# An S5 scan beside a gated MLP on one core: x tiles loaded first, transfers re-queued, and the first gate steps reordered

## The chip, the cores and the metric

The kernel runs on one core of one Trainium2 chip. The metric is the device time of one execution in microseconds; below, "us" always means that. Before the change the median of three runs is 185.41 us (185.02 to 185.9).

## The reference, cut to what matters

The input x has 2048 tokens of 448 features (bfloat16). Every token is layer-normalised to `xn`. Two branches start from `xn` and are multiplied at the end:

```
xn = layernorm(x)
h  = Lam_bar * h + xn @ B_bar.T            # complex state of 448, over the 2048 tokens
s  = 2*real(h @ C.T) + xn * Dskip
g  = silu( (sigmoid(xn @ w_gate) * (xn @ w_up)) @ w_down )      # 448 -> 1792 -> 448
out = x + s * g
```

## The kernel before, in words

**Tiles and stages.** Tokens are cut into 16 tiles of 128, and into 4 chunks of 512 (four tiles each). TensorE wants features on the partitions, so each normalised tile is transposed: in chunk 0 by TensorE itself (L495 `pe_transpose`: eight small matmuls into an accumulator `acc`, then one copy to `xnT`, by ScalarE for tile 0 and by VectorE for tiles 1 to 3), in the later chunks by DMA transposes that SyncE issues (L512). A chunk then runs through

- seven *gate steps* g0 to g6 and seven *up steps* u0 to u6 (L699 `gu_mm`): each has 7 pairs of matmuls, two halves of 64 rows side by side, into one of three double banks `gu0` to `gu2` of PSUM, taken in turn. ScalarE empties a gate step (Tanh, L721), VectorE an up step (L724). In chunk 0 all gate steps come before the up steps;
- the input side of the scan (L750 `b_phase`): it takes the next three `gu` banks and both `acc` banks. L764 and L761 are its first matmuls (part 3 into `acc`, then parts 0 and 1 into two `gu` banks), then L778 and L775; ScalarE copies the results to `bus` (L789, L795);
- the scan itself on VectorE (L826 `ssm_pair`, L862 `ssm_stack`), and the two output products `down` (L896) and `yout` (L914). Of chunk 1 on, `down` of the chunk before runs inside `b_phase`, in banks that `b_phase` has just emptied.

**Parameters.** `columns` (L535) turns three parameter rows, loaded by GpSimd, into columns with five tiny matmuls; VectorE copies them to `pv` (L546), and GpSimd and ScalarE make the scan's sine tables from it (`tables`, L570: ScalarE L575, VectorE L577 and L579, ScalarE L582 to L600). `c_scale` (L665) scales the C matrices: ScalarE L673 reads the transposed C and writes `ctmp`, VectorE L676 finishes. `skip_row` (L480) makes `xd = xn * dbc`, where `dbc` is Dskip broadcast to all partitions by a DMA.

**Loads, and names for them.** The gate weights come in three blocks for each half of the features: steps 0 and 1, steps 2 and 3, steps 4 to 6. I call them G0a, G0b, G0c for half 0 and G1a, G1b, G1c for half 1 (224, 224 and 336 KB). The up weights come in two blocks, steps 0 to 2 and 3 to 6: U0a, U0b, U1a, U1b (336 and 448 KB). A tile of x is 112 KB; "x4-7" is one DMA of four tiles. SyncE (SP) and ScalarE (ACT) issue them; every DMA of these two engines signals one of eight completion semaphores in turn, so the issue of a DMA waits for the landing of the one eight places before it. After its loads SP issues `dbc`, then the DMA transposes of B, of chunk 1's `xn`, the loads of w_down, the DMA transposes of C, and x of chunks 2 and 3.

**What sets the order.** The kernel is written down as a list of operations with costs, engines, reads and writes (L85 `add`). A planner (L138 `solve`) walks backward from TensorE's order for due times and then forward: each engine takes, of the operations that it thinks ready, the one due first. A DMA counts as landed by a rate that is written into each load (`rate=`). What comes out is one fixed order for each engine; on the chip an instruction that waits holds up all that stands behind it on its engine. While `pl.seq` is set, VectorE's order is that of the text.

Of the kernel before, what the change touches and what calls it, by code (L numbers as in the profile page):

```python
# [14 lines left out]
ACT = mybir.ActivationFunctionType  # L15
# [5 lines left out]
P = 128  # L21
H = 64
# [4 lines left out]
TPC = L // P  # L27
# [35 lines left out]
def act(n, ap=0):  # L63
    return 0.05 + 0.000833 * n + 0.093 * ap
# [181 lines left out]
def kernel(  # L246
# [18 lines left out]
    V, A, G, T, Q = nc.vector, nc.scalar, nc.gpsimd, nc.tensor, nc.sync  # L265
# [23 lines left out]
    xnT = [flat(t[:], 7, L) for t in xnT_raw]  # L289
# [28 lines left out]
    ident = sbt("ident", [P])  # L318
# [43 lines left out]
    def load_w(eng, k, half, b, r=(), rate=105e3):  # L362
        m0, m1 = BLK[k][b]
        ps = slice(half * H, half * H + H)
        c0 = half * 896
        load(eng, [("w", k, half, m) for m in range(m0, m1)], H * 7 * (m1 - m0) * P * 2,
             wgt[k][ps, :, m0 * P:m1 * P],
             wsrc[k][:, c0 + m0 * P:c0 + m1 * P].rearrange("(s p) f -> p s f", p=H), cost=0.65, r=r, rate=rate)

    def load_wd(h):  # L370
        fs = slice(h * 7, h * 7 + 7)
# [11 lines left out]
    def load_p(eng, k, r=()):  # L383
        load(eng, ("vrow", k), D * 2, vrow[k:k + 1, :], (A_log_dt, A_Lambda_im, A_Lambda_re)[k].unsqueeze(0), cost=0.75, r=r)
    load_x(0, 1, "SP")
    load_w("SP", "g", 0, 0, rate=90e3)
    load_w("SP", "g", 0, 1)
    load_x(1, 1, "ACT")
    load_x(2, 2, "ACT")
    load_w("ACT", "g", 1, 0, rate=90e3)  # L390
    load_w("SP", "g", 0, 2)
    load_w("ACT", "g", 1, 1)
    load_w("ACT", "g", 1, 2)
    load_p("POOL", 0)
    load_p("POOL", 1)
    load_p("POOL", 2)
# [7 lines left out]
    add("POOL", 0.1, lambda: G.memset(pio2[:], PI / 2), w=["pio2"])  # L404
    add("POOL", 0.6, lambda: G.iota(iota[:, 0:NTAB], pattern=[[1, NTAB]], base=0, channel_multiplier=0,
                                    allow_small_or_imprecise_dtypes=True), w=[("wv", 0)])
    for h in range(2):
        load_w("SP", "u", h, 0, rate=215e3)
    load_x(4, 4, rate=140e3)
    for h in range(2):  # L410
        load_w("SP", "u", h, 1, rate=260e3)
    load("SP", "dbc", P * D * 2, dbc[:], A_Dskip.unsqueeze(0).to_broadcast((P, D)))


# [80 lines left out]
    def pe_transpose(t):  # L495
        b, a, js = t % NXN, next_acc(), slice(t * P, t * P + P)
        tp = flat(acc[a][:].bitcast(BF16)[:, 0:7 * P], 7, P)

        def f():
            for s in range(6):  # L500
                T.transpose(tp[:, s, :], xn[b][:, s * H:s * H + P], ident[:, :])  # L501
            T.transpose(tp[0:H, 6, :], xn[b][:, 384:448], ident[:, :])
            T.transpose(tp[H:P, 6, :], xn[b][:, 0:H], ident[:, :])
        add("PE", 0.46, f, r=[("xn", b), "ident"], w=[("acc", a)])
        if t == 0:
            add("ACT", 0.85, lambda: A.copy(out=xnT[0][:, :, js], in_=tp[:, :, :]),
                r=[("acc", a)], w=[("xnT", 0, t, "a"), ("xnT", 0, t, "b")])
        else:
            add("DVE", 0.64, lambda: V.tensor_copy(out=xnT[0][:, :, js], in_=tp[:, :, :]),
                r=[("acc", a)], w=[("xnT", 0, t, "a"), ("xnT", 0, t, "b")])  # L510
# [9 lines left out]
    def xr(c, lo=0, hi=TPC):  # L520
        return [("xnT", c % 3, j, h) for j in range(lo, hi) for h in "ab"]
# [11 lines left out]


    def columns(a):  # L535
        vps = flat(gu[a][:, 0, 0:12], 4, 3)

        def f():
            for i in range(3):
                T.matmul(vps[:, i, :], lhsT=vrow[:, i * P:(i + 1) * P], rhs=ident[0:3, 0:3], start=True, stop=True)  # L540
            for h in range(2):
                T.matmul(vps[h * H:h * H + H, 3, :], lhsT=vrow[:, 384:448], rhs=ident[0:3, 0:3], start=True, stop=True)
        add("PE", 0.4, f, r=["ident"] + [("vrow", k) for k in range(3)], w=[("gu", a)])
# [154 lines left out]

    def gu_mm(c, k, m, a, lo, hi, first):  # L699
        x = xnT[c % 3]  # L700
        ts = slice(lo * P, hi * P)
        w_ = wgt[k]
        ms = slice(m * P, m * P + P)

        def f():
            for s in range(7):
                T.matmul(gu[a][:, 0, ts], lhsT=w_[0:H, s, ms], rhs=x[0:H, s, ts], start=(s == 0), stop=(s == 6))  # L707
                T.matmul(gu[a][:, 1, ts], lhsT=w_[H:P, (s + 1) % 7, ms], rhs=x[H:P, s, ts],  # L708
                         start=(s == 0), stop=(s == 6))
        n = (hi - lo) * P  # L710
        return add("PE", 7 * (0.0028 + n / 2400.0) + (2 * SW if first else 0), f,
                   r=xr(c, lo, hi) + [("w", k, 0, m), ("w", k, 1, m)], w=[("gu", a)], name=f"{k}{c}.{m}")

    sg_n = [0]

    def gu_evac(c, k, m, a):
        b = m % NSIG
        th, tk = (hF[1][:, m, :, :], ("hF", 1, m)) if c == 0 else (sig[b][:], ("sig", b))
        ho, hk = hF[c % 2][:, m, :, :], ("hF", c % 2, m)
        if k == "g":  # L720
            add("ACT", act(1024), lambda: A.activation(th, gu[a][:], ACT.Tanh, scale=0.5),  # L721
                r=[("gu", a)], w=[tk])
        else:
            add("DVE", dve1(1024), lambda: V.scalar_tensor_tensor(out=ho, in0=th, scalar=1.0, in1=gu[a][:],  # L724
                                                                 op0=ALU.add, op1=ALU.mult),
                r=[("gu", a), tk], w=[hk])
# [368 lines left out]
```

## Time and profile before, and how to read it

| | |
|---|---|
| median of 3 runs | 185.41 us (185.02, 185.41, 185.9) |
| span of the profiled execution, first to last instruction | 183.7 us |
| lies around the span (185.41 - 183.7) | 1.7 us |
| granted TensorE clock over the span | 1.00 |
| moved by DMA | 13.44 MB, mean 73 GB/s over the span |
| loads issued in the first 13.3 us: x0 to x7, gate and up weights, dbc | all landed by 22.67 us |

The page gives one execution: busy times of each engine, a chain of work that ended last, and groups of instructions by line. Two other views are used here. The timeline lists instructions in order of time as "start us, duration us, engine line operation output<-inputs xcount [idle before]"; neighbouring instructions overlap a little at their ends, so what one instruction costs in a row of many is the step from its start to the next start. The view of DMAs lists an issue with its size and the time from issue to landing; cut to a short window it shows single DMAs.

### The profile page before, as it was taken

To read this page: it belongs to the slowest core of one execution; us is meant where nothing else is said; L and a number is where in the kernel's file an instruction comes from. 1 tells how busy PE (TensorE), PEld (TensorE's weight loads), DVE (VectorE), ACT (ScalarE), POOL (GpSimd) and SP (SyncE) were. 2 spreads that over 40 slices of the span, in tenths; PEclk is the share of its full clock that TensorE was granted. 3 is DMA by queue.
4 is the path that set the end of the run, shared out by engine and by line. 5 is a ranking of instruction groups with operands and counts; after the bars stand their busy time and mean duration, and the time that the engine had idled before them with its cause. 6 is when DMAs were issued, how large, how long until landed. Compare 5 with 4: busy or idle time off the path is not lost.

```text
span 183.7 us, 3601 instructions
## 1 busy us (share of the span) xinstructions
PE 177.4 (97%) x1402; PEld 90.4 (49%) x1402; DVE 166.4 (91%) x296; ACT 94.8 (52%) x152; POOL 34.2 (19%) x95
## 2 busy tenths in 40 slices
PE   7699999999999999999999999999999999999992
PEld 2585555465554444455554444444555444455551
DVE  3873899899999998999999999999999998999973
ACT  3689993958599978665310452367120445211100
POOL 7370465000048557700000000000000000000000
PEclk9999999999999999999999999999999999999999
DMA  5999994489801370243000000002000000001121
GB/s 137 255 225 223 155 166 90 90 256 266 231 0 26 74 82 21 50 82 71 0 2 0 29 0 0 4 0 75 0 4 0 25 25 5 25 0 52 57 73 50
DMA packets 30258, 13.44 MB, mean 73 GB/s; under 512 B 19744, under 2 KB 30240, under 8 KB 30240
## 3 DMA queue, kind: packets, MB, share of 16 engines
q1 hardware_dynamic: 28336, 12.05, 30.7%
q10 hardware_dynamic: 1808, 1.15, 2.5%
q8 instruction: 11, 0.18, 0.4%
q14 instruction: 7, 0.06, 0.1%
q0 software_dynamic: 96, 0.00, 0.0%
HBM read 6.77 MB, written 1.84 MB: 47 GB/s over the span
## 4 chain that ended last, share of the span: by engine, by line
PE 93%; DMA 3%; DVE 1%; issue 1%; POOL 1%; DVEq 0%; POOLq 0%
PE gu L707 45%; PE gu L903 14%; PE acc L932 11%; PE acc L903 9%; PE gu L775 8%; DMA hF<-in_A_Lambda_re_dram 3%; PE gu L708 2%; PE acc L778 2%; PE gu L761 2%; POOL hF L353 1%; PE acc L501 0%; DVE o_t L948 0%; PE acc L764 0%; DVE o_t L944 0%; DVE o_t L941 0%
## 5 line engine op out<-in xcount | busy, mean ns | idle before, releaser
L708 PE MATMUL gu<-xnT,wG 64*128 64x512 bf16 (+2 forms) x245 | 46.0, 333 | 0.0
L707 PE MATMUL gu<-xnT,wG 64*128 64x512 bf16 (+2 forms) x245 | 46.0, 333 | 0.0
L707 PE MATMUL gu<-xnT,wU 64*128 64x512 bf16 x196 | 45.8, 376 | 0.0
L708 PE MATMUL gu<-xnT,wU 64*128 64x512 bf16 x196 | 45.8, 376 | 0.0
L721 ACT ACTIVATE sig<-gu 128x1024 f32<-128x1024 f32 x21 | 21.3, 1021 | 22.0 <-PE gu L708 21.9
L903 PEld LDWEIGHTS <-hF 128*128 128x128 bf16 x224 | 21.9, 98 | 20.7 <-issue 0.2
L707 PEld LDWEIGHTS <-wG 64*128 64x128 bf16 x245 | 21.9, 94 | 18.7
L707 PEld LDWEIGHTS <-wU 64*128 64x128 bf16 x196 | 18.4, 94 | 22.1
L724 DVE SCALAR_TENSOR_TENSOR hF<-sig,gu 128x1024 bf16<-128x1024 f32 x21 | 25.5, 1216 | 2.9 <-PE gu L708 1.6
L903 PE MATMUL gu<-wd,hF 128*128 128x448 bf16 x140 | 27.9, 352 | 0.0
L842 DVE TENSOR_TENSOR_SCAN wv<-c_r,st,z 128x512 bf16<-128x512 f32 x18 | 22.9, 1276 | 0.0
L932 PE MATMUL acc<-cT,hT 128*128 128x448 bf16 (+1 forms) x112 | 22.6, 346 | 0.0
L708 PEld LDWEIGHTS <-wG 64*128 64x128 bf16 x245 | 21.8, 94 | 0.0
L909 ACT ACTIVATE g_t<-gu 128x448 bf16<-128x448 f32 x10 | 5.4, 541 | 29.2 <-DVE o_t L946 12.9
L708 PEld LDWEIGHTS <-wU 64*128 64x128 bf16 x196 | 18.4, 94 | 0.0
L789 ACT CAST bus<-gu 128x1024 bf16<-128x1024 f32 x12 | 11.9, 1011 | 12.4 <-PE gu L761 12.2
L903 PE MATMUL acc<-wd,hF 128*128 128x448 bf16 x84 | 16.9, 352 | 0.0
L775 PE MATMUL gu<-xnT,bT 128*128 128x512 bf16 x72 | 16.7, 379 | 0.0
L932 PEld LDWEIGHTS <-hT 128*128 128x128 bf16 x119 | 11.5, 98 | 10.1 <-issue 0.4
L424 DVE BATCH_NORM_STATS2 bst<-x_all 128x6 f32<-128x448 bf16 x12 | 7.0, 610 | 5.7 <-DMA x_all<-in_A_x_dram 5.7
L795 ACT CAST bus<-acc 64x256 bf16<-64x256 f32 (+1 forms) x24 | 8.8, 369 | 6.4 <-PE acc L778 6.1
L944 DVE TENSOR_TENSOR o_t<-acc,xd 128x448 bf16<-128x448 f32 (+1 forms) x16 | 9.6, 601 | 1.3 <-PE acc L932 1.2
(138 smaller groups left out, 240.1 us busy)
## 6 DMA issues: line engine op xcount, KB each, us to landing
out_dram<-o_t SPq DMA_DIRECT2D x15, 112.0 KB, 1.7
wd<-in_B_w_down_dram SPq DMA_DIRECT2D x2, 784.0 KB, 5.5
x_all<-in_A_x_dram SPq DMA_DIRECT2D x3, 448.0 KB, 4.5
wU<-in_B_w_up_dram SPq DMA_DIRECT2D x2, 448.0 KB, 12.2
wU<-in_B_w_up_dram SPq DMA_DIRECT2D x2, 336.0 KB, 7.6
wG<-in_B_w_gate_dram SPq DMA_DIRECT2D x2, 224.0 KB, 6.5
wG<-in_B_w_gate_dram ACTq DMA_DIRECT2D x2, 224.0 KB, 6.6
xnT<-xn SPq DMA_TRANSPOSE x24, 2.4
```

The lines of the kernel that those rows point to most:

```text
L424: add("DVE", 0.6, lambda: V.bn_stats(out=bst[b][:], in_=x_all[:, t, :]), r=[("x", t)], w=[("bst", b)])
L707: T.matmul(gu[a][:, 0, ts], lhsT=w_[0:H, s, ms], rhs=x[0:H, s, ts], start=(s == 0), stop=(s == 6))
L708: T.matmul(gu[a][:, 1, ts], lhsT=w_[H:P, (s + 1) % 7, ms], rhs=x[H:P, s, ts], start=(s == 0), stop=(s == 6))
L721: add("ACT", act(1024), lambda: A.activation(th, gu[a][:], ACT.Tanh, scale=0.5), r=[("gu", a)], w=[tk])
L724: add("DVE", dve1(1024), lambda: V.scalar_tensor_tensor(out=ho, in0=th, scalar=1.0, in1=gu[a][:], op0=ALU.add, op1=ALU.mult), r=[("gu", a) ...
L775: T.matmul(gu[slots[pt]][:, i, :], lhsT=bT[:, kt, i, pt * P:pt * P + P], rhs=x[:, 2 * kt, :], start=(first and kt == 0), stop=(not first a ...
L789: add("ACT", act(1024), lambda: A.copy(out=bus[u][:], in_=gu[slots[pt]][:]), r=key(pt), w=[("bus", u)])
L795: add("ACT", 0.3, lambda ns=ns, d=d, q=q, l=l, i=i: A.copy(out=bus[u][d, l, ns], in_=acc[a3[i]][q, 0:256]), r=[("acc", a3[i])] + ([("bus", ...
L842: dve(1.194, lambda k=k: V.tensor_tensor_scan(out=wv[:, k, :], data0=rb, data1=z[:, k, :], initial=(st[pt][:, k, :] if c else 0.0), op0=AL ...
L903: T.matmul(d, lhsT=hF[c % 2][:, m, h, js], rhs=wd[:, ft, :], start=(ft == 0), stop=(ft == FT - 1))
L932: T.matmul(y, lhsT=hT[c % 2][:, hm, js], rhs=cT[:, cm, c0:c1], start=(i == 0 and not on_pe), stop=(i == 6))
L944: add("DVE", dve1(n), lambda od=od, y=y, c0=c0, c1=c1: V.tensor_tensor(out=od, in0=y, in1=xq[:, c0:c1], op=ALU.add), r=[key, ("xd", q)], w ...
```

## The change

Six edits, all in the head of the kernel (chunk 0) and the order of its loads:

1. The loads. SP: x0, x2, G0a, G0b, x4-7, G0c, U0a, U0b, U1b, dbc. ACT: x1, x3, G1a, G1b, then G1c after tile 1's standard deviation and U1a after tile 2's. Before, SP had x0, G0a, G0b, G0c, U0a, U1a, x4-7, U0b, U1b, dbc, and ACT x1, x2 and x3 in one, G1a, G1b, G1c. The rates given to the planner change too.
2. Tile 2's chain comes ahead of tile 3's statistics on VectorE; tile 2's transposed copy goes from VectorE to ScalarE; tile 4's statistics come in front of the rest.
3. `columns` goes from a place ahead of the first gate matmul to one behind g1's first half, into `acc1` instead of `gu2`; its copy goes from VectorE to ScalarE.
4. The partial gate steps are cut otherwise: before, g0 and g1 of tiles 0 and 1 one tile at a time (four parts of 128 columns), then g0, g1 and g2 of tiles 2 and 3 together, g2 of tiles 0 and 1 together. After, g0 of tile 0, g0 of tile 1, g1 of both, `columns`, the transposes of tile 2, g2 of tiles 0 and 1, the transposes of tile 3, then g0 and g1 of tile 2, g0 and g1 of tile 3, one tile at a time, and g2 of both.
5. g3 runs in the two `acc` banks instead of a `gu` bank, with two Tanh of 512 columns in place of one of 1024; so every later step takes another `gu` bank than before.
6. All else is planned anew with these, so that the fixed orders of VectorE, ScalarE and GpSimd change, in chunk 1 too.

```diff
-    load_w("SP", "g", 0, 0, rate=90e3)
-    load_w("SP", "g", 0, 1)
     load_x(1, 1, "ACT")
-    load_x(2, 2, "ACT")
-    load_w("ACT", "g", 1, 0, rate=90e3)
-    load_w("SP", "g", 0, 2)
-    load_w("ACT", "g", 1, 1)
-    load_w("ACT", "g", 1, 2)
+    load_x(2, 1, "SP", rate=180e3)
+    load_x(3, 1, "ACT", rate=180e3)
+    load_w("SP", "g", 0, 0, rate=115e3)
+    load_w("ACT", "g", 1, 0, rate=115e3)
+    load_w("SP", "g", 0, 1, rate=165e3)
+    load_w("ACT", "g", 1, 1, rate=165e3)
+    load_x(4, 4, rate=230e3)
+    load_w("SP", "g", 0, 2, rate=150e3)
...
-    for h in range(2):
-        load_w("SP", "u", h, 0, rate=215e3)
-    load_x(4, 4, rate=140e3)
-    for h in range(2):
-        load_w("SP", "u", h, 1, rate=260e3)
+    load_w("SP", "u", 0, 0, rate=150e3, slot=11)
+    load_w("SP", "u", 0, 1, rate=200e3, slot=13)
+    load_w("SP", "u", 1, 1, rate=200e3, slot=14)
     load("SP", "dbc", P * D * 2, dbc[:], A_Dskip.unsqueeze(0).to_broadcast((P, D)))
...
-        if t == 0:
+        if t in (0, 2):
             add("ACT", 0.85, lambda: A.copy(out=xnT[0][:, :, js], in_=tp[:, :, :]),
...
-        vps = flat(gu[a][:, 0, 0:12], 4, 3)
+        vps = flat(acc[a][:, 0:12], 4, 3)
...
-        add("DVE", 0.1, lambda: V.tensor_copy(out=pv[:].rearrange("p k i -> p i k"), in_=vps[:]), r=[("gu", a)], w=["pv"])
+        add("ACT", 0.2, lambda: A.copy(out=pv[:].rearrange("p k i -> p i k"), in_=vps[:]), r=[("acc", a)], w=["pv"])
...
+        if a is None:
+            for i in range(2):
+                add("ACT", act(512), lambda i=i: A.activation(th[:, i, :], acc[i][:], ACT.Tanh, scale=0.5),
+                    r=[("acc", i)], w=[tk] if i == 0 else [(tk, 1)])
...
     for t in (0, 1):
         chain(t, 1)
         norm(t)
+    load_w("ACT", "g", 1, 2, rate=150e3, r=[("sd", 1)], slot=10)
     stats(2)
-    stats(3)
     slots0 = [next_gu() for _ in range(3)]
     pe_transpose(0)
     pe_transpose(1)
-    columns(slots0[2])
-    for t in (2, 3):
-        chain(t, 1)
-        norm(t)
-    for j in range(2):
-        for m in range(2):
-            gu_mm(0, "g", m, slots0[m], j, j + 1, not (j or m))
+    chain(2, 1)
+    norm(2)
+    load_w("ACT", "u", 1, 0, rate=150e3, r=[("sd", 2)], slot=12)
+    stats(3)
+    chain(3, 1)
+    norm(3)
+    gu_mm(0, "g", 0, slots0[0], 0, 1, True)
+    gu_mm(0, "g", 0, slots0[0], 1, 2, False)
+    gu_mm(0, "g", 1, slots0[1], 0, 2, False)
+    columns(1)
     pe_transpose(2)
+    gu_mm(0, "g", 2, slots0[2], 0, 2, True)
     pe_transpose(3)
     silu_table()
+    stats(4)
     pl.seq = False
-    gu_mm(0, "g", 2, slots0[2], 0, 2, True)
-    for m in range(3):
-        gu_mm(0, "g", m, slots0[m], 2, 4, False)
-        gu_evac(0, "g", m, slots0[m])
+    gu_mm(0, "g", 0, slots0[0], 2, 3, False)
+    gu_mm(0, "g", 1, slots0[1], 2, 3, False)
+    gu_mm(0, "g", 0, slots0[0], 3, 4, False)
+    gu_evac(0, "g", 0, slots0[0])
+    gu_mm(0, "g", 1, slots0[1], 3, 4, False)
+    gu_evac(0, "g", 1, slots0[1])
+    gu_mm(0, "g", 2, slots0[2], 2, 4, False)
+    gu_evac(0, "g", 2, slots0[2])
+    gu_mm(0, "g", 3, None, 0, TPC, False)
+    gu_evac(0, "g", 3, None)
...
-    for i in range(3, 13):
+    for i in range(4, 13):
         gu_step(0, i)
```

The order that the planner makes of it, on the engines that matter below (lines of the kernel before): on VectorE the six skip rows of tiles 0 to 5 (L482), the first of them waiting for `dbc`, and one table operation (L577) now stand ahead of the first up step's emptying (L724, u0). Behind that stand u1, L579, u2, the copy of L651, u3, two operations of L589, u4, one skip row, u5. Before, u0 to u5 stood ahead of all but two of the skip rows. On ScalarE the issue of U1a, which waits for G0b's landing, stands ahead of tile 3's square root (L450); and in chunk 1's `b_phase` two scalings of C (L673), the first of which waits for the transposed imaginary C, stand ahead of the copy (L789) that empties the first of the two `gu` banks, where before they stood behind both copies.

More of the change, by code (lines that the diff above doesn't have):

```diff
@@ L360, with load_w @@
     BLK = {"g": [(0, 2), (2, 4), (4, 7)], "u": [(0, 3), (3, 7)]}
-    def load_w(eng, k, half, b, r=(), rate=105e3):
+    def load_w(eng, k, half, b, r=(), rate=105e3, slot=None):
         m0, m1 = BLK[k][b]
@@ L368, in load_w @@
              wsrc[k][:, c0 + m0 * P:c0 + m1 * P].rearrange("(s p) f -> p s f", p=H), cost=0.65, r=r, rate=rate)
+        if slot is not None:
+            pl.ops[-1].slot = slot
     def load_wd(h):
@@ L423, in stats @@
         b = t % 3
-        add("DVE", 0.6, lambda: V.bn_stats(out=bst[b][:], in_=x_all[:, t, :]), r=[("x", t)], w=[("bst", b)])
+        add("DVE", 0.6, lambda: V.bn_stats(out=bst[b][:], in_=x_all[:, t, :]),
+            r=[("x", t)] + ([("xnT", 0, 3, "a")] if 4 < t < 8 else []), w=[("bst", b)])
         add("DVE", 0.16, lambda: V.bn_aggr(out=mv[:, t, :], in_=bst[b][:]), r=[("bst", b)], w=[("mv", t)])
@@ L542, in f @@
                 T.matmul(vps[h * H:h * H + H, 3, :], lhsT=vrow[:, 384:448], rhs=ident[0:3, 0:3], start=True, stop=True)
-        add("PE", 0.4, f, r=["ident"] + [("vrow", k) for k in range(3)], w=[("gu", a)])
+        add("PE", 0.4, f, r=["ident"] + [("vrow", k) for k in range(3)], w=[("acc", a)])
         pv = sbt("pv", [3, 4], FP32)
         dt_b = C("dt", 4, BF16)
-        add("DVE", 0.1, lambda: V.tensor_copy(out=pv[:].rearrange("p k i -> p i k"), in_=vps[:]), r=[("gu", a)], w=["pv"])
+        add("ACT", 0.2, lambda: A.copy(out=pv[:].rearrange("p k i -> p i k"), in_=vps[:]), r=[("acc", a)], w=["pv"])
         dt_b = C("dt", 4, BF16)
@@ L567, in silu_table @@
     def silu_table():
-        add("ACT", 1.3, lambda: A.preload_act_table_set("silu_and_others"), r=[("sd", t) for t in range(4)], w=["silutab"])
+        add("ACT", 1.3, lambda: A.preload_act_table_set("silu_and_others"), r=[("sd", t) for t in range(4)] + [("xnT", 0, 2, "a")], w=["silutab"])
     def tables():
@@ L700, in gu_mm @@
         x = xnT[c % 3]
+        bank, keys = ([gu[a][:, 0, :], gu[a][:, 1, :]], [("gu", a)]) if a is not None else (
+            [acc[0][:], acc[1][:]], [("acc", 0), ("acc", 1)])
         ts = slice(lo * P, hi * P)
@@ L706, in f @@
             for s in range(7):
-                T.matmul(gu[a][:, 0, ts], lhsT=w_[0:H, s, ms], rhs=x[0:H, s, ts], start=(s == 0), stop=(s == 6))
-                T.matmul(gu[a][:, 1, ts], lhsT=w_[H:P, (s + 1) % 7, ms], rhs=x[H:P, s, ts],
+                T.matmul(bank[0][:, ts], lhsT=w_[0:H, s, ms], rhs=x[0:H, s, ts], start=(s == 0), stop=(s == 6))
+                T.matmul(bank[1][:, ts], lhsT=w_[H:P, (s + 1) % 7, ms], rhs=x[H:P, s, ts],
                          start=(s == 0), stop=(s == 6))
@@ L711, in gu_mm @@
         return add("PE", 7 * (0.0028 + n / 2400.0) + (2 * SW if first else 0), f,
-                   r=xr(c, lo, hi) + [("w", k, 0, m), ("w", k, 1, m)], w=[("gu", a)], name=f"{k}{c}.{m}")
+                   r=xr(c, lo, hi) + [("w", k, 0, m), ("w", k, 1, m)], w=keys, name=f"{k}{c}.{m}")
     sg_n = [0]
@@ L719, in gu_evac @@
         ho, hk = hF[c % 2][:, m, :, :], ("hF", c % 2, m)
-        if k == "g":
+        if a is None:
+            for i in range(2):
+                add("ACT", act(512), lambda i=i: A.activation(th[:, i, :], acc[i][:], ACT.Tanh, scale=0.5),
+                    r=[("acc", i)], w=[tk] if i == 0 else [(tk, 1)])
+        elif k == "g":
             add("ACT", act(1024), lambda: A.activation(th, gu[a][:], ACT.Tanh, scale=0.5),
@@ L725, in gu_evac @@
                                                                  op0=ALU.add, op1=ALU.mult),
-                r=[("gu", a), tk], w=[hk])
+                r=[("gu", a), tk] + ([(tk, 1)] if (tk, 1) in pl.w else []), w=[hk])
     def gu_step(c, i, first=False):
@@ L993, in stats_for @@
             if c not in (3,):
-                stats(t)
+                if t != 4:
+                    stats(t)
             elif t % 2:
```

## The prediction

> **What bounds the kernel now.** I read the engines' busy times first, then what TensorE waited for over the whole span, then the chain of waits, then the head engine by engine.
>
> ```profile
> PE 177.4 (97%) x1402; PEld 90.4 (49%) x1402; DVE 166.4 (91%) x296; ACT 94.8 (52%) x152; POOL 34.2 (19%) x95
> ```
> ```profile
> PE gu L418 <- DVE hF L378: 1.2, 1, 1.2
> PE gu L540 <- DMA hF<-in_A_Lambda_re_dram: 1.0, 1, 1.0
> PE acc L501 <- DVE xn L469: 0.5, 1, 0.5
> ```
>
> The second fence is all that TensorE waits for in 183.7 us, and all of it lies before 7.63 us. From there it never stands still. So the time is 7.63, then a stream of fixed length, then the last stores. The change removes no matmul. It can gain only what the stream starts earlier, and every new wait behind 7.63 is paid in full, since no later slack takes it up.
>
> ```profile
> 2.53 4.96 DMA hF<-in_A_Lambda_re_dram
> 7.49 0.14 issue
> 7.63 0.21 PE gu L540 x3
> 7.84 0.12 PE gu L542 x2
> 7.96 0.16 PE gu L707
> ```
>
> This is the chain's start: the last parameter row lands at 7.49, `columns` runs, the first gate matmul follows. I measure below in **lag**: how much later than before TensorE reaches the same amount of work. The final lag is the largest that any wait forces.
>
> **The start (lag -0.2).** With `columns` moved back, g0 waits for tile 0's copy (L506, 6.07+0.91 = 6.98) and for G0a and G1a, which landed at 1.18+5.9 = 7.08 and 1.68+5.9 = 7.55. Ahead of those two stand the same four x tiles, now split evenly over the two queues; I take 7.4. The work ahead of g4, 7.63 to 15.38, is unchanged, so the lag is 7.4-7.63 = -0.2. Bounds: -0.6 (g0 right behind the copy, 7.05) and 0.
>
> **Instructions (0).** The order built from the changed text has 14 matmuls more, not fewer: 14 pairs of 128 columns come for 7 of 256. The timeline steps 0.055 us for the one and 0.109 for the other: 14 x 0.055 - 7 x 0.109 = +0.01. Two Tanh of 512 (bounded by 0.54 of L909 and 1.04 of L721 each) replace one of 1.04, off the path: the banks `acc` that they free are next needed at 30.5. The `pv` copy (0.18 on VectorE, at most 0.37 by L795 on ScalarE) stands ahead of tile 2's copy, which is not needed until tile 3's transposes are through. Tile 2's copy itself (0.91 for 0.6) likewise.
>
> **ScalarE's issue of U1a (lag +0.3).** In the built order this DMA waits for G0b's landing and has tile 3's square root behind it, so tile 3's reciprocal, normalisation and transposes wait too. G0b landed at 1.96+7.1 = 9.1, G1b at 2.44+7.4 = 9.8; with x2 now ahead of G0b I take 9.4. Then issue 0.65 (L353 rows), square root to reciprocal 0.44 (4.76 to 5.20), 0.26 to the normalisation, 0.45 from it to TensorE: 11.2. TensorE would be there at 10.65 (7.4 + 0.39+0.39+0.77+0.33+0.62+0.77). That turns -0.2 into +0.3; with G0b at 9.0 it is -0.1, at 9.8 it is +0.7.
>
> **G0c behind x4-7 (lag +0.3 to +0.8).** g4 needs G0c at 15.7. SP now has x4-7 (448 KB) ahead of it, which took 3.2 us from U1a's landing (15.8) to its own (19.0). Counting bytes on both queues from 9.4 at 249 GB/s, G0c lands at about 15.5, at 222 GB/s at 16.2. I take +0.3.
>
> **Skip rows ahead of the up steps (lag +2.1, the likeliest end).** This one decides. `dbc` is the last of the head's loads:
>
> ```profile
> dbc<-in_A_Dskip_dram SPq DMA_DIRECT2D x1, 112.0 KB, 11.5
> ```
> ```profile
> 4.50:11.00 6.50, 5.03 (x101) 3.90 (x100) 4.84 (x18) 3.94 (x7) 2.88 (x12) 1.00 1.09 249
> 11.50:20.00 8.50, 8.50 (x106) 5.62 (x102) 4.81 (x12) 8.50 (x12) 1.84 (x4) 1.00 1.23 222
> ```
>
> It was issued at 11.18 and landed at 22.67. The last column of the two stages is GB/s: the DMA engines were full all along (shares 1.09 and 1.23), at 249 while both queues had loads and at 222 with SP alone. The changed text moves the same 4.2 MB in another order, and `dbc` stays last on SP. ACT has work until about 14 instead of 11.5, which by these rates is worth 2.5 x 27 = 68 KB or 0.3 us; with some evenness I take 22.2. Bounds: 22.7 (no gain) and 20.1 (the 345 GB/s that the stage 38 to 42 shows, from 14 on). The Trainium skill, "DMA: Bandwidth & Descriptors", section "Issuing engines are not separate DMA queues", says that issuing from several engines saves only the issuing time; by it `dbc` lands at 22.67 and the lag would be 2.6 in place of 2.1.
>
> VectorE reaches the first skip row before that. x4-7 lands at about 13.5, and the statistics and tables ahead of it need some 6 us. Then VectorE stands still until `dbc`, and up steps u0 to u5 are behind it. Prices:
>
> ```profile
> 12.45 0.69 DVE L579 SCALAR_TENSOR_TENSOR hT<-hT,hT 128x513 f32<-128x513 f32 x1
> 13.05 0.42 DVE L577 TENSOR_SCALAR hT<-hT 128x513 f32<-128x513 f32 x1
> ...
> 27.43 0.49 DVE L589 TENSOR_SCALAR spm<-spm 128x512 bf16<-128x512 bf16 x2
> 27.83 1.22 DVE L724 SCALAR_TENSOR_TENSOR hF<-hF,gu 128x1024 bf16<-128x1024 bf16 x1
> 28.96 0.39 DVE L482 TENSOR_TENSOR xd<-xn,dbc 128x448 bf16<-128x448 bf16 x1
> 29.27 1.21 DVE L724 SCALAR_TENSOR_TENSOR hF<-hF,gu 128x1024 bf16<-128x1024 bf16 x1
> 30.40 0.39 DVE L482 TENSOR_TENSOR xd<-xn,dbc 128x448 bf16<-128x448 bf16 x1
> ...
> 32.07 1.89 DVE L482 TENSOR_TENSOR xd<-xn,dbc 128x448 bf16<-128x448 bf16 x6
> ```
>
> By steps from start to start: six skip rows 1.85, L577 0.36, an up step 1.13 (27.83 to 28.96), L579 0.60, L651 0.30, two L589 0.40, a skip row 0.31. u0 is emptied at 22.2+1.85+0.36+1.21 = 25.6. TensorE wants its bank for u3 at 24.43 (19.91 + 3 x 1.51): lag 1.2. The chain goes on to the end of u5: 22.2 + 1.85+0.36+1.13+1.13+0.60+1.13+0.30+1.13+0.40+1.13+0.31+1.21 = 32.9. u5's bank is now that of part 1 of `b_phase`, whose matmul (L761, the second pair) stood at 30.82 before:
>
> ```profile
> 30.49 0.29 PE L764 MATMUL acc<-xnT,bT 64*128 64x256 bf16 x2
> 30.60 0.61 PE L761 MATMUL gu<-xnT,bT 64*128 64x512 bf16 x4
> ```
>
> With 0.06 for the signal the lag is 32.94-30.82 = **2.1**. Before, u5 was emptied at 30.45, 0.4 ahead of need, because `dbc` was waited for behind it. The rule for bounds: each us on `dbc` is a us on the lag, 2.6 at 22.7 and 0 at 20.1.
>
> **C's scalings ahead of a bank's copy (lag +1.5, covered).** In chunk 1's `b_phase` ScalarE now waits for the imaginary C, landed at 42.80+4.1 = 46.9, before it empties part 0's bank, which `down` wants at 47.29. SP's row of transposes follows the head's loads, so I take 46.5: two scalings 1.2, copy 1.0, so 48.75 and a lag of 1.5 (1.9 at 46.9). A lag of 2.1 from the skip rows covers it. Behind `b_phase` VectorE's lists hold the same operations, and both sides are late together: 0, or up to +0.7 if VectorE, busy 91%, empties one bank late by the length of a C scaling (L676, 0.68).
>
> **The sum.** -0.2, then +0.3, +0.3, +2.1: they don't add, the largest counts. 183.7+2.1 = 185.8 for the profiled execution. The runs' median lies 1.7 above the span, so 185.41+2.1 = **187.5 us**.
>
> **Rivals.**
> - *The loads are through earlier.* If `dbc` lands by 20.1, the skip rows cost nothing and the start decides: 185.41-0.2 = 185.2 with the issue of U1a in time, 184.8 at the bound, 185.7 with the +0.3. For it: the stage 38 to 42 shows 345 GB/s, so the engines can do more than the head shows. Against it: no stretch of the head after 4.5 us shows that rate over several us. This is the case on the other side (not slower). The point from which it decides is `dbc` 2 us earlier; nothing in the change can gain more than 0.6 us (0.3%).
> - *The C wait is the end.* `dbc` lands at about 21 but SP's transposes don't move: 185.41+1.5 = 186.9.
> - *More than the skip rows.* `dbc` at 22.7 or later, and +0.7 from a bank behind: 185.41+2.6+0.3 = 188.3, at most 188.8.
> - *The change doesn't do what it says.* Fewer TensorE instructions it doesn't bring (+14); by the 0.01 above that is worth nothing by itself.
>
> **How the numbers follow.** Skip rows, +1.5 to +2.6: 0.60. C wait, or `dbc` at about 21, +0.9 to +1.5: 0.12. More, to +3.4: 0.10. Loads earlier, -0.6 to +0.9: 0.18. A measurement tells 0.5%, 0.93 us, from no change. Faster by more than that: 0.02, for something I don't see; within: 0.17; slower: 0.81. The range leaves out the upper tail behind 188.5 and the lower half of the early case: 185.7 to 188.5.
>
> **What would show it.** VectorE idle some 2 us or more in front of a skip row (L482 of before) with `dbc` named as what ended it; TensorE's first wait behind the start in u3 and a second at L761 of the first `b_phase`, both put down to VectorE's emptying; the square root of tile 3 at about 10; SP's transposes as late as before. I am wrong if `dbc` lands before 21, if TensorE runs through from 8 to 179 without a wait, or if waits of more than 0.3 us turn up behind chunk 1.

## The result, and the profile after

The changed kernel takes **188.29 us** (median of 4 runs: 188.3, 188.42, 188.27, 186.9) where the kernel before takes 185.27 beside it (185.02 to 185.9): a ratio of **1.0132**, 95% interval 1.0093 to 1.0171. The prediction was 187.5. A few executions of some kernels below were in a slower state: the ratios leave those out, the medians hold them. The profiled execution has a span of 186.53 against 183.68: 2.85 later, 1.8 around it. In the changed kernel line numbers are 2 to 8 higher: L484 is the skip row, L711 and L712 the two halves of a gate or up matmul, L732 the up emptying, L769 `b_phase`'s first matmul, L675 the C scaling, L797 the copy of a `gu` bank.

The place to read first is what TensorE waited for in the whole span (total, times, longest):

```profile
PE gu L712 <- DMA wU<-in_B_w_up_dram: 1.7, 1, 1.7
PE gu L419 <- DVE hF L380: 1.2, 1, 1.2
PE gu L711 <- DMA wG<-in_B_w_gate_dram: 0.7, 1, 0.7
PE acc L503 <- DVE xn L471: 0.4, 1, 0.4
```

Before, nothing was waited for after 7.63. Now the largest wait is for an *up weight*, `wU`, a load that the sum of the prediction did not hold. The chain of waits of the same execution shows which (start, duration):

```profile
2.42 7.55 DMA wG<-in_B_w_gate_dram
9.99 12.76 DMA wU<-in_B_w_up_dram
34.89 3.88 PE gu L783 x18
```

G0b, issued at 2.42, lands at 9.97; 0.02 later ScalarE issues U1a, whose semaphore G0b held; and U1a takes 12.76, to 22.75. Before, SP issued it at 7.74 and it landed at 15.82, 8.1 later:

```profile
wU<-in_B_w_up_dram SPq DMA_DIRECT2D x1, 336.0 KB, 8.1
```

TensorE needs it for u0:

```profile
20.76 0.38 PE L711 MATMUL gu<-xnT,wU 64*128 64x512 bf16 x1
22.80 0.39 PE L712 MATMUL gu<-xnT,wU 64*128 64x512 bf16 x1 [1.67 <-DMA wU<-in_B_w_up_dram]
22.80 0.39 PE L711 MATMUL gu<-xnT,wU 64*128 64x512 bf16 x1
```

The first half of u0 starts at 20.76, its partner from half 1 stands until 22.80. The predicted wait is there too. VectorE's timeline (idle before an instruction in brackets):

```profile
20.04 0.17 DVE L631 RECIPROCAL c_inv<-c_den 128x4 f32<-128x4 f32 x1
22.92 1.90 DVE L484 TENSOR_TENSOR xd<-xn,dbc 128x448 bf16<-128x448 bf16 x6 [2.72 <-DMA dbc<-in_A_Dskip_dram]
24.74 0.42 DVE L579 TENSOR_SCALAR hT<-hT 128x513 f32<-128x513 f32 x1
25.07 2.35 DVE L732 SCALAR_TENSOR_TENSOR hF<-hF,gu 128x1024 bf16<-128x1024 bf16 x2
...
32.47 1.21 DVE L732 SCALAR_TENSOR_TENSOR hF<-hF,gu 128x1024 bf16<-128x1024 bf16 x1
```

Idle for 2.72, six skip rows behind `dbc` (22.90), and u5 emptied at 33.68. The second pair of L769 starts at 33.73, against 30.82 before: lag 2.92. But TensorE was already 2.68 late when U1a had landed, so what comes behind it adds only 0.24, too little for the table. Even of that, 0.19 rises one matmul earlier, at the partner of the first pair, and rises there in e2 and e5 too, where no skip row is late; the wait for u5's bank itself adds 0.05. **Two waits lie one on the other, and either alone would explain nearly the whole loss.** From there on the lag stays at 2.91 to the last output product.

The stages of the loads (last columns: granted clock, DMA share, GB/s) have changed little: the same bytes at nearly the same rate, 249 and 222 before.

```profile
4.50:11.00 6.50, 5.72 (x87) 4.07 (x87) 3.76 (x14) 1.76 (x6) 0.55 (x3) 1.00 1.10 255
11.50:20.00 8.50, 8.30 (x128) 5.67 (x130) 6.63 (x20) 8.47 (x12) 5.49 (x16) 1.00 1.12 216
```

### The profile page after: what moved, and what is told of

The parts are those of the page before. It is cut to its first block, busy times and chain, and to the rows that moved or that the text cites. A ratio compares the mean times of both kernels' runs of the same rounds, so it can differ in the third digit from the quotient of the medians.

```text
span 186.5 us, 3632 instructions
## 1 busy us (share of the span) xinstructions
PE 179.0 (96%) x1416; PEld 89.8 (48%) x1416; DVE 165.4 (89%) x294; ACT 95.3 (51%) x155; POOL 33.1 (18%) x95
## 4 chain that ended last, share of the span: by engine, by line
PE 85%; DMA 11%; SPq 1%; DVE 1%; issue 0%; DVEq 0%
PE gu L711 34%; PE gu L911 14%; PE acc L940 11%; PE acc L911 9%; PE gu L783 8%; DMA wU<-in_B_w_up_dram 7%; PE gu L712 6%; DMA wG<-in_B_w_gate_dram 4%; PE gu L769 2%; PE acc L786 2%; SPq L353 1%; DVE o_t L956 0%; DVE o_t L952 0%; DVE o_t L949 0%; PE acc L772 0%
## 5 line engine op out<-in xcount | busy, mean ns | idle before, releaser
L712 PE MATMUL gu<-xnT,wU 64*128 64x512 bf16 x196 | 45.8, 377 | 1.7 <-DMA wU<-in_B_w_up_dram 1.7
L711 PE MATMUL gu<-xnT,wU 64*128 64x512 bf16 x196 | 46.0, 376 | 0.0
L711 PE MATMUL gu<-xnT,wG 64*128 64x512 bf16 (+2 forms) x245 | 44.9, 328 | 0.7 <-DMA wG<-in_B_w_gate_dram 0.7
L712 PE MATMUL gu<-xnT,wG 64*128 64x512 bf16 (+2 forms) x245 | 44.9, 328 | 0.0
L711 PEld LDWEIGHTS <-wG 64*128 64x128 bf16 x252 | 21.9, 94 | 19.7 <-DMA wG<-in_B_w_gate_dram 0.9
L732 DVE SCALAR_TENSOR_TENSOR hF<-sig,gu 128x1024 bf16<-128x1024 f32 x21 | 25.5, 1215 | 2.7 <-PE gu L712 1.4
L711 PEld LDWEIGHTS <-wU 64*128 64x128 bf16 x196 | 18.4, 94 | 17.1
L712 PEld LDWEIGHTS <-wU 64*128 64x128 bf16 x196 | 18.4, 94 | 7.7 <-DMA wU<-in_B_w_up_dram 2.2
L712 PEld LDWEIGHTS <-wG 64*128 64x128 bf16 x252 | 21.9, 94 | 0.0
L797 ACT CAST bus<-gu 128x1024 bf16<-128x1024 f32 x12 | 11.9, 1008 | 12.3 <-PE gu L769 12.2
L940 PEld LDWEIGHTS <-hT 128*128 128x128 bf16 x119 | 11.5, 98 | 10.1 <-issue 0.4
L783 PEld LDWEIGHTS <-bT 128*128 128x128 bf16 x72 | 7.0, 98 | 7.5
```

Of the source, the lines that this page charges most:

```text
L711: T.matmul(bank[0][:, ts], lhsT=w_[0:H, s, ms], rhs=x[0:H, s, ts], start=(s == 0), stop=(s == 6))
L712: T.matmul(bank[1][:, ts], lhsT=w_[H:P, (s + 1) % 7, ms], rhs=x[H:P, s, ts], start=(s == 0), stop=(s == 6))
L783: T.matmul(gu[slots[pt]][:, i, :], lhsT=bT[:, kt, i, pt * P:pt * P + P], rhs=x[:, 2 * kt, :], start=(first and kt == 0), stop=(not first a ...
L797: add("ACT", act(1024), lambda: A.copy(out=bus[u][:], in_=gu[slots[pt]][:]), r=key(pt), w=[("bus", u)])
L940: T.matmul(y, lhsT=hT[c % 2][:, hm, js], rhs=cT[:, cm, c0:c1], start=(i == 0 and not on_pe), stop=(i == 6))
```

## The experiments

Theories at the start: *two waits beside each other*, U1a's landing and the skip rows behind `dbc`, with the C scalings in ScalarE's list (the prediction's "C wait") as a third close behind. Rivals: one alone is the cause; or the reordered head itself costs time. Each ratio is against runs of the kernel before on the same chip. Lags are read from each profiled execution against that of the kernel before.

| kernel | U1a / dbc / imaginary C landed | lag at g3 | at u1 | second pair of first b_phase | chunk 2 on | span | median (runs) | ratio, 95% |
|---|---|---|---|---|---|---|---|---|
| before | 15.8 / 22.67 / 46.89 | 0 | 0 | 0 | 0 | 183.7 | | 1 |
| changed | 22.75 / 22.90 / 47.15 | 0.84 | 2.68 | 2.92 | 2.91 | 186.5 | 188.29 (4) | 1.0132 (1.0093-1.0171) |
| e1 U1a on SP | 17.15 / 21.50 / 46.10 | -0.04 | -0.04 | 1.52 | 1.67 | 185.3 | 187.96 (10) | 1.0099 (1.0050-1.0148) |
| e2 skip rows late | 21.73 / 21.61 / 46.94 | 0.48 | 1.66 | 1.72 | 2.53 | 186.1 | 188.59 (10) | 1.0134 (1.0093-1.0174) |
| e3 both | 17.96 / 22.27 / 46.54 | 0.29 | 0.29 | 0.49 | 2.13 | 185.8 | 187.12 (10) | 1.0034 (0.9995-1.0073) |
| e4 both, copies ahead of C | 17.43 / 21.67 / 48.55 | 0.27 | 0.27 | 0.47 | 3.96, then 6.83 | 190.4 | 189.75 (4) | 1.0156 (1.0064-1.0248) |
| e5 order of before, U1a on ACT | 20.90 / 21.87 / 47.20 | 0.43 | 0.83 | 0.94 | 1.02 | 184.6 | 187.40 (10) | 1.0058 (1.0010-1.0106) |
| e7 as e5, U0a on ACT | U0a 20.26 / 21.15 / 46.05 | -0.40 | 0.40 | 0.40 | 0.38 | 184.0 | 186.69 (10) | 1.0058 (1.0017-1.0099) |
| e8 true rates | 17.20 / 21.80 / 46.34 | 0.03 | 0.03 | 0.24 | 0.24 | 183.9 | 185.83 (12) | 1.0016 (0.9987-1.0044) |
| e9 before, false rates | 14.81 / 21.63 / 45.56 | -0.43 | 1.80 | 2.12 | 2.12 | 185.8 | 187.54 (12) | 1.0103 (1.0068-1.0137) |
| e10 x3 later | 20.76 / 24.18 / 50.18 | 0.60 | 0.82 | 0.82 | 1.85 | 185.5 | 187.29 (12) | 1.0074 (1.0038-1.0110) |

The same bytes are through at 21.15 to 22.90 in different executions (e10 apart). A kernel that waits for the last load repeats that in its time; so a single profiled execution and a median may differ by 1 us, and I read each wait from the trace and each price from both.

### e1: U1a issued by SP

```diff
+    at[55].fn = lambda: Q.dma_start(out=wgt["u"][H0, :, 0:3 * P], ...)   # U1a
+    move(55, behind=26)                                                  # behind U0a
```

> The changed kernel with one DMA moved: U1a is issued by SP right behind U0a, no longer by ACT behind tile 2's standard deviation. In the changed kernel's trace TensorE stood 1.74 us at u0 until U1a landed at 22.75, and VectorE stood 2.72 us in front of the skip rows until dbc landed at 22.90. Theory (two waits of nearly the same lag, U1a at 2.7 and the skip rows at 2.9): U1a lands at about 17 to 19, TensorE's wait at u0 is gone, but dbc stays last and lands at 22.7 to 22.9, so the lag comes back in u3 and at the second pair of the first b_phase and the time is 187.7 to 188.3. Rival (U1a's wait is the cause and the skip rows only hide behind it): 186.0 to 186.6. Second rival (a load's place in the order of issue is not what sets its landing; the shared rate is): U1a lands above 20 although it is issued earlier.

U1a lands at 17.15, u0 waits for nothing, tile 3's square root runs at 8.66 in place of 10.64, and the lag at g3 is gone. It comes back as expected: VectorE waits for `dbc` (21.50 here), and TensorE for u5's bank:

```profile
30.98 0.29 PE L772 MATMUL acc<-xnT,bT 64*128 64x256 bf16 x2
31.09 0.40 PE L769 MATMUL gu<-xnT,bT 64*128 64x512 bf16 x2
32.33 0.39 PE L769 MATMUL gu<-xnT,bT 64*128 64x512 bf16 x2 [0.85 <-DVE hF L732]
```

`dbc` is 1.40 earlier than in the changed kernel, and the lag there 1.40 smaller (1.52 for 2.92): the prediction's rule "each us on `dbc` is a us on the lag" to the hundredth. The median, 187.96, says that U1a is not the cause by itself; both rivals fall.

### e2: the six skip rows behind u6

```diff
+    for idx in (130, 125, 106, 105, 104, 103):   # the six early skip rows
+        move(idx, behind=266)                    # behind the emptying of u6
```

> The changed kernel with VectorE's six early skip rows moved behind the emptying of u6, where they stood before the change; U1a stays on ACT. Theory (two waits): U1a still lands at about 22.7 and u0 waits for it, lag 2.7 from there on and no second wait at the first b_phase, so 187.9 to 188.2, 0.1 to 0.4 below the changed kernel. Rival (the skip rows alone make the loss): the start and tile 3's square root decide, lag 0.8, 186.0 to 186.3.

One wait at u0, as U1a lands (21.73): lag 1.66. So the skip rows alone are not the cause either, and the median, 188.59, is no better than the changed kernel's; it lies above the range that I had expected. I had also expected no wait behind it, and there are two: 0.2 in chunk 1's `down` and 0.46 behind it, lag 2.07 and then 2.53. Both are ScalarE's.

### e3: both

```diff
+    move(55, behind=26)                          # as e1, issued by SP
+    for idx in (130, 125, 106, 105, 104, 103):
+        move(idx, behind=266)
```

> Both edits: U1a issued by SP behind U0a, and the six skip rows behind the emptying of u6. Theory with the C wait of the prediction behind the two: the lag is 0.3 to 0.8 up to the end of the first b_phase, then ScalarE waits for the transposed imaginary C (landed at 47.15 in the changed kernel) ahead of the bank's copy in chunk 1 and the lag rises to 2.0 to 2.3: 187.2 to 187.6. Rival (the C wait is not real, the bank is free in time): 185.5 to 186.2.

The C wait is real, by the trace: the time alone does not tell this kernel from no change (ratio 1.0034, 0.9995 to 1.0073). What TensorE waited for, and ScalarE's timeline in chunk 1's `b_phase`:

```profile
PE gu L419 <- DVE hF L380: 1.2, 1, 1.2
PE gu L911 <- ACT bus L797: 1.0, 1, 1.0
PE gu L711 <- ACT bus L797: 0.3, 1, 0.3
```
```profile
46.63 0.67 ACT L675 ACTIVATE ctmp<-xnT,c_n2i 128x448 f32<-128x448 bf16 x1 [2.86 <-DMA xnT<-in_A_C_im_dram]
47.20 0.65 ACT L675 ACTIVATE ctmp<-xnT,c_n2r 128x448 f32<-128x448 bf16 x1
47.76 0.99 ACT L797 CAST bus<-gu 128x1024 bf16<-128x1024 f32 x1
```

ScalarE stands 2.86 with a bank full in front of it, because a scaling whose C is not there is ahead in its list. The bank is free at 48.75, `down` starts at 48.80 (lag 1.68). The third bank's copy, behind more of the same list, comes at 60.78 and is late again: lag 2.13. With a lag of 0.49 already there at the first `b_phase`, this third wait adds 1.64.

### e4: the two copies ahead of the C scalings

```diff
+    move(376, ahead=282)     # the two L797 copies
+    move(378, ahead=282)     # ahead of the first L675
```

> As before it, and in chunk 1's b_phase ScalarE's two copies that empty the gu banks stand ahead of its scalings of C, as they did before the change. Theory (three waits, U1a, skip rows, C): the start and tile 3's square root alone are left, lag 0.2 to 0.8, 185.5 to 186.1. Rival (something else in the changed order is late as well): 186.5 or more.

Missed: 189.75. The first bank is now in time (0.47 at the second pair, 0.46 at `down`), but the third bank's copy still stands behind the whole row of C work, and imaginary C landed at 48.55 in this execution:

```profile
PE gu L711 <- ACT bus L797: 3.3, 1, 3.3
```

```profile
59.96 0.38 PE L711 MATMUL gu<-xnT,wG 64*128 64x512 bf16 x1
63.67 0.58 PE L711 MATMUL gu<-xnT,wU 64*128 64x512 bf16 x1 [3.34 <-ACT bus L797]
```

During that wait the granted clock (first of the last three columns) fell: at 62.66, 2.3 us after the last matmul's end at 60.34, and it stayed at 0.50 until 69.49. The wait ends with ScalarE's copy, so its length does not come from TensorE's clock: the first matmul behind it starts at a lag of 3.96. The rest of the 6.83 is matmuls at half the clock and belongs to no order of instructions. C landed 2 us later here than in e3 although it was issued at nearly the same time (42.58 and 42.30); why, I did not find.

```profile
60.00:61.00 1.00, 0.34 (x4) 0.05 (x1) 1.00 (x2) 0.65 (x3) 0.91 (x3) 1.00 0.00 0
61.00:62.00 1.00, 0.00 (x0) 0.00 (x0) 1.00 (x4) 0.68 (x2) 0.92 (x3) 1.00 0.64 131
62.00:63.00 1.00, 0.00 (x0) 0.00 (x0) 1.00 (x2) 1.00 (x3) 1.00 (x1) 0.83 0.41 95
63.00:64.00 1.00, 0.33 (x2) 0.13 (x3) 1.00 (x2) 1.00 (x2) 0.56 (x4) 0.50 0.11 20
...
69.00:70.00 1.00, 1.00 (x10) 0.41 (x8) 0.45 (x1) 0.24 (x1) 1.00 (x2) 0.76 0.65 131
70.00:71.00 1.00, 1.00 (x12) 0.52 (x10) 0.00 (x0) 1.00 (x2) 0.76 (x4) 1.00 0.42 98
```

So the two swaps were not enough, and I changed the theory: ScalarE's list in chunk 1, not two instructions of it.

**What the four give together.** Each wait is a straight line in one landing, fitted in one execution and found again in the others:

- U1a: lag at u1 = landing - 20.07. From the changed kernel (22.75, 2.68). e2: 21.73, 1.66 measured; e5 below: 20.90, 0.83 measured.
- dbc: lag at the second pair = landing - 19.98. From the changed kernel; e1: 21.50, 1.52 measured.
- C: lag from chunk 1's up steps on = landing - 44.41. From e3 (46.54, 2.13); e2: 46.94, 2.53 measured; e1: 46.10, 1.69 for 1.67 measured.

In the changed kernel's execution they give 2.68, 2.92 and 47.15 - 44.41 = 2.74. Three waits within 0.25 us of each other, in three places, by three loads. No run tells whether the evenness is chance; what I looked for was something that the three share, and that is the plan. By its own rule (a queue for each engine, each load at its written rate) it counted landings as follows, in its own time:

| | planned before | landed before | planned after | landed after |
|---|---|---|---|---|
| U1a | 14.5 | 15.8 | 11.8 | 22.75 |
| dbc | 21.8 | 22.67 | 18.8 | 22.90 |
| imaginary C | 47.3 | 46.89 | 43.0 | 47.15 |

The change's `rate=` numbers and the loads moved to ACT bring the plan 2.7 to 4.3 us forward. On the chip `dbc` and C landed 0.2 and 0.3 later than before, and U1a 6.9 later. New theory: **the loss is this one error, seen three times**; the order of the head itself is harmless.

### e5: the order of before, U1a left on ACT

The emission follows a fixed list: the six skip rows late, and from the first scan operation on the order of before on VectorE, ScalarE and GpSimd.

```diff
-        pl.emit()
+        for k in ORDER:
+            at[k].fn()
```

> The changed kernel's loads and head, U1a on ACT as the change has it; the six early skip rows behind the emptying of u6, and from the first scan operation on, VectorE, ScalarE and GpSimd in the order that they had before the change (the C scalings behind the two copies of banks, and all that stands behind them as before too). Theory (U1a, skip rows and ScalarE's row behind C are three waits beside each other, and only U1a is left here): one wait at u0, as long as U1a's landing is late: lag 1.7 if it lands at 21.7, 2.7 if at 22.75; no second wait behind; 187.0 to 188.0. Rival (the reordered chunk 1 was not what raised the lag from 1.66 to 2.5 with the late skip rows): the lag rises again behind the first b_phase by 0.4 or more.

One wait at u0 (U1a at 20.90, lag 0.83), and 1.02 at the end: C at 47.20 does no harm in the old order. The ratio of 1.0058 (1.0010 to 1.0106) makes U1a alone worth some 1.1 us (0.2 to 2.0). By the straight line it is worth 2.68 where it lands at 22.75, as in the changed kernel's own profile.

### e8: the planner told the true landings

```diff
-    load_w("SP", "g", 0, 0, rate=115e3)
-    load_w("ACT", "g", 1, 0, rate=115e3)
-    load_w("SP", "g", 0, 1, rate=165e3)
-    load_w("ACT", "g", 1, 1, rate=165e3)
+    load_w("SP", "g", 0, 0, rate=65e3)
+    load_w("ACT", "g", 1, 0, rate=70e3)
+    load_w("SP", "g", 0, 1, rate=109e3)
+    load_w("ACT", "g", 1, 1, rate=127e3)
...
-    load_w("SP", "u", 0, 0, rate=150e3, slot=11)
-    load_w("SP", "u", 0, 1, rate=200e3, slot=13)
+    load_w("SP", "u", 0, 0, rate=164e3, slot=11)
+    load_w("SP", "u", 1, 0, rate=191e3, slot=12)
+    load_w("SP", "u", 0, 1, rate=191e3, slot=13)
...
-    load_w("ACT", "g", 1, 2, rate=150e3, r=[("sd", 1)], slot=10)
+    load_w("ACT", "g", 1, 2, rate=64e3, r=[("sd", 1)], slot=10)
...
-    load_w("ACT", "u", 1, 0, rate=150e3, r=[("sd", 2)], slot=12)
```

> The changed kernel's text with U1a among SP's loads and six rate numbers changed, so that the planner counts the loads as landed when the chip landed them (dbc at 22.8 in its own time in place of 18.8, imaginary C at 47.0 in place of 43.0). Nothing is moved by hand. Theory (the loss is one error seen in three places: the changed rates tell the planner that the head's loads are through 4 us earlier than they are, and it puts skip rows, C scalings and the rest ahead of work that is wanted sooner): it puts them back by itself, lag 0 to 0.5, 185.3 to 186.0. Rival (the order of the head itself, columns, parts and accumulators, costs time): 186.5 or more.

(Eight numbers in fact, U1a's among them.) All that TensorE waits for:

```profile
PE gu L420 <- DVE hF L380: 1.2, 1, 1.2
PE gu L712 <- DMA wG<-in_B_w_gate_dram: 0.5, 1, 0.5
```

The planner itself puts the skip rows (L485 here) behind u6 and the C scalings (L676) behind the copies (L798):

```profile
31.25 1.21 DVE L733 SCALAR_TENSOR_TENSOR hF<-hF,gu 128x1024 bf16<-128x1024 bf16 x1
32.59 1.89 DVE L485 TENSOR_TENSOR xd<-xn,dbc 128x448 bf16<-128x448 bf16 x6
```
```profile
45.35 1.01 ACT L798 CAST bus<-gu 128x1024 bf16<-128x1024 f32 x1
46.42 0.67 ACT L676 ACTIVATE ctmp<-xnT,c_n2i 128x448 f32<-128x448 bf16 x1
```

185.83, ratio 1.0016 (0.9987 to 1.0044): the loss is gone within what this can tell, with the changed head, the columns, the parts and the accumulators all in place. They are worth nothing either way that this can tell.

The edit does two things, though: beside the rates it gives U1a back to SP. e1 did that alone. So the rates are tested by e8 beside e1 (185.83 for 187.96, a final lag of 0.24 for 1.67), and what they take away is the waits for `dbc` and for C. For U1a, e1 shows that its place in the loads makes its wait; that true rates would remove this wait with U1a left on ACT was not tried. "One error, seen three times" is shown for two of the three.

### e9: the kernel before, told false rates

```diff
-    load_w("SP", "g", 0, 2)
+    load_w("SP", "g", 0, 2, rate=150e3)
...
-        load_w("SP", "u", h, 0, rate=215e3)
-    load_x(4, 4, rate=140e3)
+        load_w("SP", "u", h, 0, rate=285e3)
+    load_x(4, 4, rate=210e3)
...
-        load_w("SP", "u", h, 1, rate=260e3)
+        load_w("SP", "u", h, 1, rate=285e3)
```

> The kernel before, its loads and queues untouched, with four rate numbers raised so that the planner believes dbc landed at 18.6 (21.8 before) and imaginary C at 44.0 (47.3 before). It then puts six skip rows ahead of u0's emptying and scalings of C ahead of the second bank's copy, as in the changed kernel. Theory (order made for transfers that come too early is the loss): dbc lands at 22.7 as before, VectorE waits for it ahead of u0's emptying, u5's bank is late at the first b_phase by 22.67 + 1.85 + 6 up steps and small ones to 32.7 against 30.82, lag about 1.9; 187.0 to 187.8. Rival (the new loads and not the order make the loss): 185.2 to 185.9, no wait.

187.54, ratio 1.0103 (1.0068 to 1.0137): with no load moved, four false numbers make most of the same loss. The size was expected; the place was not. TensorE's only late wait is in u1, for ScalarE:

```profile
20.80 0.38 PE L708 MATMUL gu<-xnT,wU 64*128 64x512 bf16 x1
23.22 0.37 PE L707 MATMUL gu<-xnT,wU 64*128 64x512 bf16 x1 [2.05 <-ACT hF L721]
```
```profile
20.85 1.41 ACT L474 ACTIVATE xn<-x_all,nmr,rsd 128x448 bf16<-128x448 bf16 x2 [1.74 <-DVE nmr L459]
22.17 1.00 ACT L721 ACTIVATE hF<-gu 128x1024 bf16<-128x1024 f32 x1
```

The false plan counted x4-7 as landed at 14.9; it came at 17.87. So its normalisations stand ahead of a Tanh on ScalarE and wait, and the Tanh's bank with them. The skip rows add 0.32 behind that. Same error, in another place.

### e7: U0a on ACT in place of U1a

```diff
+    at[26].fn = lambda: A.dma_start(out=wgt["u"][0:H, :, 0:3 * P], ...)   # U0a by ACT
+    at[55].fn = lambda: Q.dma_start(out=wgt["u"][H0, :, 0:3 * P], ...)    # U1a by SP
```

> As the kernel with the order of before, but U1a issued by SP and U0a in its place by ACT, behind tile 2's standard deviation, at about 7.5 to 8 (its completion semaphore is free when G0a has landed, not G0b). Theory (a load flows in the order of issue over both queues, so what made U1a late was its issue at 10, behind U0b, U1b and dbc, and not ACT's queue): U0a lands at 14.5 to 17.5 and TensorE does not wait at u0; lag 0 to 0.5, 185.3 to 186.0. Rival (a transfer on ACT's queue is held back while SP's queue is full): U0a lands above 19, TensorE waits for it at u0.

Missed as to the landing: 20.26, with a wait of 0.6 at u0, which is the rival's number. But its issue was not where I had meant it: it waited for G0b (7.96) after all, so U0b (7.16) and U1b (7.83) were issued ahead of it, and it landed behind U0b (18.86) and 0.71 ahead of U1b (20.97). By itself e7 does not separate the two ideas; e5 does. There U1a was issued by ACT at 8.64, between SP's U0b (8.15) and U1b (8.82), and landed at 20.90, between 19.77 and 21.68. A queue that is held back while SP's is full should have landed it behind U1b.

### e10: a better start?

```diff
-    load_x(2, 1, "SP", rate=180e3)
-    load_x(3, 1, "ACT", rate=180e3)
-    load_w("SP", "g", 0, 0, rate=65e3)
+    load_x(2, 1, "ACT", rate=180e3)
+    load_w("SP", "g", 0, 0, rate=61e3)
+    load_x(3, 1, "SP", rate=180e3)
```

> As the kernel with the measured rates, and x3 goes from ACT, where it stood ahead of G1a, to SP behind G0a; x2 goes to ACT. So G0a and G1a have one tile of x less ahead of them. Theory (loads flow in the order of issue over both queues): G0a and G1a land 112 KB or about 0.4 earlier, at 6.6 to 7.0, x3 lands behind them at 7.0 to 7.7, in time for its statistics at 7.8; TensorE starts g0 at about 7.0 in place of 7.4, lag -0.4 to 0, 184.9 to 185.5, which would be the best of all kernels here by a little. Rival (the start is not the only limit of the head, or the weights land no earlier): the same as with the measured rates, 185.5 to 186.1.

Missed: of G0a and G1a the later one landed no earlier (7.08 and 7.74, in e8 7.42 and 7.00), x3 only at 8.43, and the time is 187.29. The head accounts for 0.60 of the lag of 1.85, at g3. Most of the rest comes from something that I had not looked at. SP's timeline of issues:

```profile
3.29 0.72 SPq L353 DMA_DIRECT2D x_all<-in_A_x_dram  x1
7.10 0.61 SPq L353 DMA_DIRECT2D wG<-in_B_w_gate_dram  x1
7.75 4.35 SPq L353 DMA_DIRECT2D wU<-in_B_w_up_dram  x4
```

G0c is issued at 7.10 and not at 4.05: with x2 moved to ACT, G0a is one place earlier and is now the load eight places before G0c, and G0c waits for its landing (7.08). All behind it slides, `dbc` to 24.18, SP's transposes and chunk 1's `xn` with it, where TensorE waits 0.8. No version here beats the kernel before.

## Why the prediction was right, and where it was not

- **The wait that decides.** Skip rows behind `dbc`: right in mechanism, place (the second pair of L769) and slope, as e1 shows where U1a is out of the way. In the changed kernel itself it decided only the last 0.05, since U1a's wait came first. Its size was off by the landing above all: I took 22.2 and bounded it at 22.7; it came at 22.90, which is 0.7 of the 0.8 between 2.1 and 2.92. The reason given, ACT "has work until about 14", was wrong: ACT had a load on its way until 22.75, and the stage from 11.5 to 20 still ran at 216 GB/s, not at the 249 that I took for two queues. The rule of the Trainium skill, "DMA: Bandwidth & Descriptors", section "Issuing engines are not separate DMA queues", which I weighed and did not take, would have given 22.67 and 2.6. The trace (22.90) stands on its side. (The bound of 20.1 does not come out of its own numbers either: 14 + 8.67 x 222/345 = 19.6. Nothing rests on the difference, as the skip rows cost nothing at either.)
- **The missing term.** I priced what ScalarE's issue of U1a does to tile 3 and not when U1a itself lands. At the issue time that I took, 9.4, with U0b and U1b issued ahead of it and the engines full, the bytes that I counted for `dbc` say "among the last": it landed at 22.75, a lag of 2.68. That nearly equals the skip rows' 2.92, so the sum was still right within 0.8, by luck: waits that take the place of each other do not add. The rival "More than the skip rows" names 188.3, the measured time, and its first half (`dbc` at 22.7 or later) came true; its second, a bank late behind, did not: the lag stays at 2.91.
- **The issue of U1a for tile 3** (+0.3, +0.7 if G0b at 9.8): G0b at 9.97, square root at 10.64, TensorE waits 0.40 at tile 3, lag 0.84 at g3. Right in mechanism; G0b and the lag came 0.2 and 0.1 beyond the bad bound.
- **The start** (-0.2): G0a landed at 7.76, g0 began at 7.81 and not at 7.4: +0.2. In e8, with the same loads at the start, it landed at 7.42.
- **G0c behind x4-7** (+0.3 to +0.8): wrong. It landed at 13.49, not 15.5: it was issued at 4.06, far ahead of the up weights, and no wait followed.
- **Instructions** (0): borne out by e8, lag 0.03 at g3 and 0.24 in the end with all of them.
- **C's scalings** (+1.5, 1.9 at 46.9, covered): covered, yes, but by less than thought. At 47.15 the first bank alone gives 2.3 (e3: 46.54, 1.68) and the bank behind 2.74. The first bank's size was short by 0.17 because I took `down`'s start from the chain (47.29), where the timeline has its first matmul at 47.12. My "+0.7 by VectorE" was 0.46 by ScalarE.
- **What would show it.** VectorE's idle (2.72) and SP's transposes (first of chunk 1's `xn` at 25.26, before 25.22) as said; the first wait was in u0 and for a load, not in u3 and for VectorE.

Left open: why the loads take 21.15 to 22.90 for the same bytes from one execution to the next, why C came so late in e4, what true rates would do with U1a left on ACT, and how much of e9's loss each of its two waits holds alone; none of these was tried.

## What to carry to other kernels

Where a planner lays a fixed order by assumed landings, check those landings against the trace before anything else: an optimistic rate moves no transfer, and in e9 four of them alone put waiting instructions in front of due work on VectorE and ScalarE (ratio 1.0103). A load moved to a second queue did not come sooner here; price each by the bytes issued ahead of it on *both* queues, and by the completion semaphore that it takes over. When removing one wait gains nothing, look for a second of the same length before calling the first harmless.

## What was not expected of the hardware

- The loads issued from 6.5 us on landed nearly in the order of issue over both queues, in every kernel here (at most 0.71 us out of it, in e7): in the changed kernel U0a 7.78, U0b 8.42, U1b 9.10, dbc 9.77, U1a (alone on ACT's queue) 9.99, landed at 16.37, 19.27, 22.57, 22.90, 22.75. It does not hold for the first loads: in the kernel before x2 and x3 on ACT, issued at 1.20, landed at 5.06, and G0a on SP, issued at 1.18, at 7.08.
- Order of landing is not order of every packet. The view of DMAs of the changed kernel, cut to 14 to 16 us, has 0.41 MB on SP's queue and nothing on ACT's, where U1a was pending; from 16 to 20 it has 0.50 MB on SP's and 0.33 MB, nearly all of U1a, on ACT's. So U1a first waited some 6 us and then shared, and the total hardly rose (205 and 212 GB/s). Its last packet ran at 21.28, and it landed 1.5 later; why, no run here shows.
- After 2.05 us without a matmul in e9 the granted clock stayed at 1.00; in e4's profiled execution it fell to 0.50 after 2.3 us without one, and stayed there for 6.8 us. Behind the last matmul of a span it fell after 2.0 us (e4) to 5.0 us (before). The Trainium skill, "TensorE: Matmul & The Clock Gate", section "Part 1: The HAM clock gate (the "warmup" mystery)", puts the fall at an idle window of about 3.4 us; e9 fits that, but e4's two falls came sooner, and here the measurement decides.
- Moving a load one place in the order of issue held back another, eight places later, by 3 us (e10: 7.10 for 4.05).
